# Due times from a backward pass, head-major features, phi on GpSimd and reciprocals on ScalarE in a two-layer linear-attention and gated-MLP kernel

## The chip, the cores and the metric

The kernel runs on one core of a Trainium2 chip. The core has five engines: PE (TensorE, matmuls), DVE (VectorE), ACT (ScalarE), POOL (GpSimd) and SP (SyncE, which issues DMAs here). The metric is the device time of one execution in microseconds; smaller is better.

## The reference

The input is x of 2048 rows and 512 columns. Two layers run, each of an attention block A and a gated MLP block B, both with a residual and a LayerNorm without gain; both layers use the same weights.

```python
qkv = (x @ wqkv).reshape(B, S, 3, H, Dh)...             # H = 32 heads of Dh = 16
pq = einsum("bhsd,hdf->bhsf", q, w_phi)                 # the same for k
phi_q = concat([softmax(pq), softmax(-pq)])             # 32 features a head
kv = einsum("bhsf,bhsd->bhfd", phi_k, v);  z = sum_s phi_k
o  = (phi_q @ kv) / (phi_q @ z + 1e-6)
A  = o.reshape(B, S, D) @ wo
B  = (relu(x @ W_gate) * (x @ W_up)) @ W_down           # F = 1376
x = x + A(ln(x)); x = x + B(ln(x)); x = x + A(ln(x)); x = x + B(ln(x))
```

## The kernel before

The rows are cut into T = 16 tiles of 128. All of x (X, four pieces of four tiles), all weights and the transposed normalized rows (xnTA) stay in SBUF. w_phi is folded into the key and query weights once (`fold`, Wk2 and Wq2: four transposes of the weight on PE, then products with a block-diagonal Wblk).

For a tile of layer l the work is this, with the names under which it stands in the profile:

- `norm_A` (lines 312 to 333): stats and aggr on DVE, Ln and Exp on ACT for the reciprocal standard deviation (rsA), the normalized tile xn on DVE (line 328) or, in layer 0 from tile 2 on, on ACT (line 324, after a small product on DVE, line 321), then a DMA transpose into xnTA issued by SP.
- `Keys.tile` (lines 343 to 390): K (line 348) and V (line 354), four matmuls of 512 columns each; ek, two exponentials on ACT; vext, V copied by ACT; sk, a sum over the 16 features on DVE (line 360); rk, its reciprocal on DVE (line 366); phiK = ek * rk (line 371) on POOL in layer 0 but for the last tile, on DVE otherwise; kvz, eight matmuls of 129 columns that accumulate over all 16 tiles in three PSUM banks. The features of the keys lie feature-major: the 16 features of a head are 8 elements apart.
- `Keys.build`: R, the block-diagonal result, once all 16 tiles are summed.
- `queries`: per four tiles, four groups of four matmuls (line 419) and eight exponentials Eq on ACT. `attend` (lines 429 to 473): eight query matmuls with R (line 437), six copies by ACT (DS, N), six small operations on DVE that end in o, a DMA transpose oT, the projection with wo (line 467) and the residual resA on DVE.
- `mlp` (lines 476 to 538): works on two tiles at once. stats and the centred rows xc (written into the pool xn, line 484), two DMA transposes into xnTB, then for six pairs of the 11 column groups of F the matmuls G and Up (line 504, 256 columns), the copies rg and ru by ACT, their product hT on DVE; then `down` (line 531, 11 matmuls a tile in one piece) and the residual resB on DVE.

The order of the instructions is made by `plan` before anything is emitted. Each operation has an engine, a cost (time that it holds the engine, time until its result), a due time written by hand (TL, STEP, LEAD, ATT in lines 541 to 576), its dependences and the buffers that it takes from pools. `plan` runs a list schedule over the five engines: at every step the engine that can start first takes, among the operations that can start at that time, the one with the smallest due time. Each engine then executes its instructions strictly in that order. PSUM's eight banks are three pools: q (3), a (2: K, Q and the projection) and b (3: V, G, Up, down and the fold). SP issues all loads but wk and wv, all transposes and the stores, in one queue.

## Time and profile before

| | us |
|---|---|
| time of the runs, median of 3 | 440.36 (439.55 to 440.63) |
| the profiled execution, its own time | 439.55 |
| its span, first to last instruction | 437.8 |
| busy PE | 392.7 (90%) |
| busy DVE | 299.8 (68%) |
| busy ACT | 256.6 (59%) |
| busy POOL | 29.4 (7%) |
| mean granted TensorE clock | 0.987 |

The shares are averages over stages with different limits, so the busy time has to be read stage by stage. A row of the stage table gives a stretch of the span; where PE is busy for nearly all of a stretch, only fewer or shorter matmuls shorten it, and elsewhere the wait that ends last has to be found. The groups list all instructions of one line, engine, operation and shape together: count, busy time, the mean of one in ns, and the idle time of the engine ahead of them with its releaser. The chain of waits follows the program back from its last instruction to what released each step.

### The profile page before, as it was taken

What the parts mean: (1) busy time and instruction counts of PE and PEld (TensorE: products, weight loads), DVE (VectorE), ACT (ScalarE), POOL (GpSimd) and SP (SyncE); (2) the same over time, 40 slices, a digit from 0 to 9 for tenths busy, and PEclk for the clock granted to TensorE, in tenths of its full rate; (3) what the DMA queues carried; (4) which work ended last, traced back from release to release, by engine and by line L of the source; (5) the groups of instructions that cost most, each with busy time, mean ns of one, the idle gap of its engine ahead of it and who ended that gap; (6) DMA issues with size and microseconds to landing.
All of it is one profiled execution on the core that took longest, in us unless ns stands there. A gap on an engine that the chain in (4) does not pass through costs nothing.

```text
span 437.8 us, 7642 instructions
## 1 busy us (share of the span) xinstructions
PE 392.7 (90%) x2808; PEld 260.6 (60%) x2848; DVE 299.8 (68%) x687; ACT 256.6 (59%) x631; POOL 29.4 (7%) x21
## 2 busy tenths in 40 slices
PE   1778697899999989989999999877999999999996
PEld 1334344466867555567666654354866868677873
DVE  5599995897799997974746553389956678522222
ACT  3587797993757455554646457966624647335531
POOL 0055572000000000000000000000000000000000
PEclk9999999999999999999999999959999999999999
DMA  8982110251224220100000101003331132200000
GB/s 268 368 209 49 37 36 1 49 72 35 53 49 85 62 49 12 25 0 14 12 14 13 24 1 24 1 12 75 76 69 36 37 76 49 60 13 13 24 25 25
DMA packets 62021, 23.62 MB, mean 54 GB/s; under 512 B 53440, under 2 KB 60960, under 8 KB 61984
## 3 DMA queue, kind: packets, MB, share of 16 engines
q1 hardware_dynamic: 60928, 22.08, 21.4%
q10 hardware_dynamic: 1056, 1.05, 0.8%
q8 instruction: 22, 0.36, 0.4%
q14 instruction: 15, 0.12, 0.1%
HBM read 8.44 MB, written 2.10 MB: 24 GB/s over the span
## 4 chain that ended last, share of the span: by engine, by line
PE 55%; DVE 24%; ACT 8%; DMA 7%; issue 3%; POOL 1%; DVEq 0%; ACTq 0%; SPq 0%
PE b L504 28%; PE b L531 14%; DVE sk L360 9%; PE a L467 4%; PE a L419 3%; ACT Eq L423 3%; DVE rk L366 3%; DVE phiK L371 2%; DMA xnTA<-xn 2%; ACT ek L351 2%; PE q L382 2%; DMA wu<-in_B_W_up_dram 2%; DMA X<-in_A_x_dram 2%; PE a L348 2%; ACT N L444 2%
## 5 line engine op out<-in xcount | busy, mean ns | idle before, releaser
L504 PE MATMUL b<-xnTB,wg 128*128 128x256 bf16 (+1 forms) x704 | 92.5, 273 | 0.5 <-DMA xnTB<-xn 0.4
L504 PE MATMUL b<-xnTB,wu 128*128 128x256 bf16 (+1 forms) x704 | 92.5, 273 | 0.0
L514 ACT ACTIVATE rg<-b 128x512 bf16<-128x512 f32 x96 | 54.7, 570 | 54.4 <-PE b L504 53.6
L531 PE MATMUL b<-wd,hT 128*128 128x512 bf16 (+1 forms) x342 | 78.5, 379 | 0.8
L360 DVE TENSOR_REDUCE sk<-ek 128x64 f32<-128x1024 bf16 x32 | 63.1, 1972 | 19.9 <-ACT ek L351 19.9
L521 DVE TENSOR_TENSOR hT<-rg,ru 128x512 bf16<-128x512 bf16 x96 | 37.7, 394 | 56.6 <-ACT ru L518 56.4
L504 PEld LDWEIGHTS <-wg 128*128 128x128 bf16 (+1 forms) x704 | 69.0, 100 | 12.2 <-DMA xnTB<-xn 0.6
L504 PEld LDWEIGHTS <-wu 128*128 128x128 bf16 (+1 forms) x704 | 69.5, 100 | 9.5 <-issue 0.2
L518 ACT CAST ru<-b 128x512 bf16<-128x512 f32 x96 | 53.2, 554 | 32.7 <-PE b L504 32.2
L531 PEld LDWEIGHTS <-hT 128*128 128x128 bf16 (+1 forms) x352 | 34.4, 98 | 39.8 <-issue 0.3
L444 ACT CAST N<-q 128x384 bf16<-128x384 f32 (+1 forms) x96 | 44.2, 514 | 0.5 <-DVE pr L459 0.5
L351 ACT ACTIVATE ek<-a 128x512 bf16<-128x512 f32 x64 | 35.7, 596 | 11.6 <-PE a L348 11.6
L535 DVE SCALAR_TENSOR_TENSOR X<-b,rsB,X 128x512 bf16<-128x512 f32 x32 | 23.8, 745 | 26.7 <-PE b L531 26.7
L423 ACT ACTIVATE Eq<-a 128x512 bf16<-128x512 f32 x64 | 35.2, 634 | 6.2 <-PE a L419 5.6
L348 PE MATMUL a<-Wk,xnTA 128*128 128x512 bf16 x120 | 32.0, 384 | 5.5 <-DMA xnTA<-xn 5.1
L354 PE MATMUL b<-wv,xnTA 128*128 128x512 bf16 x124 | 33.0, 387 | 3.8 <-DMA xnTA<-xn 2.5
L419 PE MATMUL a<-xnTA,Wq 128*128 128x512 bf16 x122 | 31.3, 378 | 2.5 <-ACT Eq L423 2.1
L444 ACT COPY DS<-q 128x48 f32<-128x48 f32 (+1 forms) x96 | 24.4, 255 | 14.6 <-PE q L437 13.4
L467 PE MATMUL a<-wo,oT 128*128 128x512 bf16 x116 | 30.6, 382 | 1.1 <-DMA oT<-o 0.3
L437 PE MATMUL q<-R,Eq 128*128 128x144 bf16 x256 | 27.4, 240 | 4.6 <-ACT N L444 3.2
L382 PE MATMUL q<-vext,phiK 128*128 128x129 bf16 x256 | 20.6, 224 | 12.0 <-DVE phiK L371 9.0
L371 POOL TENSOR_TENSOR phiK<-ek,rk 128x1024 bf16<-128x1024 bf16 x15 | 28.7, 1911 | 39.0 <-DVE rk L366 27.7
(55 smaller groups left out, 360.1 us busy)
## 6 DMA issues: line engine op xcount, KB each, us to landing
out_dram<-X SPq DMA_DIRECT2D x16, 128.0 KB, 1.7
X<-in_A_x_dram SPq DMA_DIRECT2D x3, 512.0 KB, 7.2
wg<-in_B_W_gate_dram SPq DMA_DIRECT2D x4, 344.0 KB, 7.8
wu<-in_B_W_up_dram SPq DMA_DIRECT2D x4, 344.0 KB, 6.8
wd<-in_B_W_down_dram SPq DMA_DIRECT2D x5, 256.0 KB, 3.6
wk<-in_A_wqkv_dram ACTq DMA_DIRECT2D x1, 512.0 KB, 4.4
wv<-in_A_wqkv_dram ACTq DMA_DIRECT2D x1, 512.0 KB, 5.7
wq<-in_A_wqkv_dram SPq DMA_DIRECT2D x1, 512.0 KB, 7.5
```

The costliest lines, as they stand in the source:

```text
L348: k = op("PE", mm(4, 512), due, lambda: [nc.tensor.matmul(kp.t[:], lhsT=xnTA[c][:, b, cols], rhs=Wk2[:, b, :], start=(b == 0), stop=(b == ...
L351: e = [op("ACT", act(512), due, lambda s=s: nc.scalar.activation(out=ek.t[:, s, :], in_=kp.t[:], func=AF.Exp, scale=1.0 - 2.0 * s), [k], [ ...
L360: a = op("DVE", (1140, 1225), due, lambda: nc.vector.tensor_reduce(out=sk.t[:], in_=ek.t[:].rearrange("p s (b f j) -> p (s b) j f", b=NB, ...
L419: q = op("PE", mm(4, 512), due(c, b), lambda b=b, qp=qp: [nc.tensor.matmul(qp.t[:], lhsT=Wq2[:, m, b * P:(b + 1) * P], rhs=xnTA[c][:, m, : ...
L423: done.append(op("ACT", act(512), due(c, b), lambda b=b, s=s, qp=qp: nc.scalar.activation(out=Eq[c][:, b, s, :], in_=qp.t[:], func=AF.Exp, ...
L444: nc.scalar.copy(out=q[:, k, 0:3] if k < 2 else q[:, :, 3], in_=ps.t[:, 0:n * GE].rearrange("p (n c j) -> p n c j", n=n, j=HB)[:, :, lo:hi])
L467: a = op("PE", mm(4, 512), due + 3, lambda: [nc.tensor.matmul(yp.t[:], lhsT=oT.t[:, b, :], rhs=wo[:, b, :], start=(b == 0), stop=(b == NB ...
L504: nc.tensor.matmul(ps.t[:m, k * 256:(k + 1) * 256], lhsT=W[:, b, g * P:g * P + m], rhs=xT.t[:, b, :], start=(b == 0), stop=(b == NB - 1))
L514: a = op("ACT", act(256 * n), due(0, f), lambda gp=gp, rg=rg, two=two, two_ps=two_ps: nc.scalar.activation(out=two(rg), in_=two_ps(gp), fu ...
L518: u = op("ACT", act(256 * n), due(0, f), lambda up=up, ru=ru, two=two, two_ps=two_ps: nc.scalar.copy(out=two(ru), in_=two_ps(up)), [u], [r ...
L521: lambda rg=rg, ru=ru, two=two, f=f, n=n, w=w: nc.vector.tensor_tensor(out=h.t[:w, f:f + n, :], in0=two(rg), in1=two(ru), op=Alu.mult), [a ...
L531: nc.tensor.matmul(yp.t[:], lhsT=h.t[:m, f, i * P:(i + 1) * P], rhs=wd[:m, f, :], start=(f == 0), stop=(f == NF - 1))
```

## The change

**The planner.** `plan` may now be run several times on the same operations. It gives an operation the smaller due time of those that wait for a buffer of a pool that it holds, counts matmuls at twice their cost for the first 3.5 us, and keeps one clock for DMA traffic. A new function `back` runs the schedule backward, from the last operation, and sets every due time to minus the time that is left behind it; `refine` alternates `plan` and `back` eight times, keeps the due times of the shortest plan and emits that order. The hand-written due times remain as the first round's; their constants are changed, and so are a few costs.

**Features.** The 16 features of a head now lie side by side. sk reads neighbours; Ln and Exp(-x) on ACT turn sk into its reciprocal in place (fp32) instead of DVE's reciprocal; phi multiplies by that fp32 factor, repeated along the features, on POOL in both layers, and half on DVE, half on POOL for the last tile of layer 0 and the last two of layer 1.

**Transposes and norms.** `turn` transposes by DMA or by PE with a copy by ACT or DVE. PE does it for the norms of tiles 0 to 3 in layer 0 and 14 and 15 in layer 1, and for oT and xnTB of tiles 0 and 1 in both layers. xn is always made on DVE.

**MLP blocks.** A block may hold one tile (128 columns; four column groups of F share one bank) or two; the first two blocks of both layers and the last two of layer 1 hold one. `down` is emitted in three pieces, the order alone deciding what stands between them. G and Up of a pair are no longer tied to ACT's copies one by one.

**Loads and banks.** wk comes in two halves, later X in halves, and all other weights one or two pieces after each tile's norm; a warm-up of eight matmuls on zeros is added; pools a and b become one pool of five banks.

```diff
-HOP = {"PE": 50, "ACT": 30, "DVE": 30, "POOL": 165, "SP": 90}
+HOP = {"PE": 50, "ACT": 32, "DVE": 32, "POOL": 165, "SP": 90}
+COLD = 3500
 def plan(ops):
...
+        def rank(o):
+            return min([o.due] + [wanted[b.pool] for b in o.uses + o.takes if b.pool in wanted]), o.n
...
-            pick = min((o for t, o in at if t <= first + 1), key=lambda o: (o.due, o.n))
+            best = first, min((o for t, o in at if t <= first + 1), key=rank)
...
+        if o.eng == "PE":
+            warm = t + COLD if warm is None else warm
+            if t < warm:
+                occ, lat = 2 * occ, lat + occ
+        if o.move:
+            queue = max(t + 1400, queue) + o.move
+            lat = max(lat, queue + 600 - t)
...
+def back(ops):
...
+                at = [(max(clock[e], ready[o] + o.end - o.start - o.spent), o) for o in cand]
...
+        clock[o.eng] = t + o.spent
+        o.due = -clock[o.eng]
...
+def refine(ops, rounds):
...
+    for k in range(rounds):
+        dues = [o.due for o in ops]
+        span = max(o.end for o in plan(ops))
+        if best is None or span < best[0]:
+            best = span, dues
+        back(ops)
...
-POOL_PHI = (2100, 1940)
-XPOSE = (1200, 2470)
+POOL_PHI = (1930, 1940)
+XPOSE = (1200, 2430)
...
+ROUNDS = 8
+BLOCKS = ((1, 1, 2, 2, 2, 2, 2, 2, 2), (1, 1, 2, 2, 2, 2, 2, 2, 1, 1))
...
-    p_q, p_a, p_b = psum("q", 3), psum("a", 2), psum("b", 3)
+    p_q, p_b = psum("q", 3), psum("b", 5)
+    p_a = p_b
...
+    op("PE", mm(8, 512), 0, lambda: [nc.tensor.matmul(
+        wps.t[:], lhsT=p_h.tiles[0][:, 0:P], rhs=p_h.tiles[0][:, 0:512],
+        start=True, stop=True) for _ in range(8)], [c_z], [wps], name="warm")
...
+    def turn(src, dst, how, due, after, takes, uses, name):
+        if how == "SP":
+            return op("SP", XPOSE, due, lambda: nc.sync.dma_start_transpose(out=dst(), in_=src.t[:]), [after],
+                      takes, [src] + uses, name=name, move=500)
+        ps = Buf(p_b)
+        a = op("PE", mm(4, 128), due, lambda: [nc.tensor.matmul(
+            ps.t[:, b * P:(b + 1) * P], lhsT=src.t[:, b * P:(b + 1) * P], rhs=ident[:], start=True, stop=True)
+            for b in range(NB)], [after, c_id], [ps], [src], name=name)
+        return evac(how, due, dst, lambda: ps.t[:].rearrange("p (b t) -> p b t", b=NB), [a], takes, [ps] + uses,
+                    name)
...
-            a = op("DVE", (1140, 1225), due, lambda: nc.vector.tensor_reduce(
-                out=sk.t[:], in_=ek.t[:].rearrange("p s (b f j) -> p (s b) j f", b=NB, j=HB), axis=AX.X,
-                op=Alu.add), e, [sk], [ek], name="sk")
-            def recip():
-                with nc.allow_low_precision("softmax weights are bf16"):
-                    nc.vector.reciprocal(out=rk.t[:], in_=sk.t[:])
-            a = op("DVE", rcp(64), due, recip, [a], [rk], [sk], name="rk")
+            a = op("DVE", SUM16, due, lambda: nc.vector.tensor_reduce(
+                out=sk.t[:], in_=ek.t[:].rearrange("p s (h f) -> p (s h) f", f=DH), axis=AX.X, op=Alu.add), e,
+                [sk], [ek], name="sk")
+            a = op("ACT", (210, 310), due, lambda: nc.scalar.activation(
+                out=sk.t[:], in_=sk.t[:], func=AF.Ln, scale=1.0), [a], (), [sk], name="lnk")
+            a = op("ACT", (110, 220), due, lambda: nc.scalar.activation(
+                out=sk.t[:], in_=sk.t[:], func=AF.Exp, scale=-1.0), [a], (), [sk], name="rk")
+            def phi(e, s, n):
+                e.tensor_tensor(
+                    out=ph.t[:, s:s + n].rearrange("p s (h f) -> p (s h) f", f=DH),
+                    in0=ek.t[:, s:s + n].rearrange("p s (h f) -> p (s h) f", f=DH),
+                    in1=sk.t[:, s * H:(s + n) * H].unsqueeze(2).to_broadcast([P, n * H, DH]), op=Alu.mult)
...
+            for lo, hi in ((0, 4), (4, 8), (8, NF)):
+                def down(yp=yp, i=i, lo=lo, hi=hi):
...
-            nxt.append(norm_A(1, t, s0 + 14000 + 2000 * i, [a], "DVE"))
-            keys.tile(t, max(s0 + 22000 + 2500 * i, TL[0] + ATT * T + 3000 * t), nxt[t], "DVE")
+                    nxt.append(norm_A(1, t, e0 + 2400 * i, [a], "ACT" if t >= T - 2 else "SP"))
+                    keys.tile(t, k0, k0 + p["V0"], k0 + p["Z0"], nxt[t], "POOL" if t < T - 2 else "BOTH",
+                              "DVE" if t >= T - 1 else "ACT")
...
-    order = plan(ops)
+    order = refine(ops, ROUNDS)
```

What the new order does to the queues is shown at three places. The first is SP's queue in the load stage. Before, from the third piece of the gate weight on (wg and wu are the gate and up weights, wo the output weight; the number behind a name is that of a buffer, so xnTA_80 is one of the four pieces of the transposed rows):

```order
L227 DMA wg<-in_B_W_gate_dram 128x1376
L332 DMA_TRANSPOSE xnTA_80<-xn_114 128x4x128
L227 DMA wg<-in_B_W_gate_dram 128x1376
L227 DMA wu<-in_B_W_up_dram 128x1376 x2
L332 DMA_TRANSPOSE xnTA_80<-xn_115 128x4x128
L227 DMA wu<-in_B_W_up_dram 128x1376 x2
L227 DMA wo<-in_A_wo_dram 32x4x512 x4
```

and in the changed kernel, the first transposes on that queue:

```order
L379 DMA_TRANSPOSE xnTA_80<-xn_114 128x4x128
L298 DMA wq<-in_A_wqkv_dram 128x512 x2
L379 DMA_TRANSPOSE xnTA_80<-xn_115 128x4x128
L298 DMA wg<-in_B_W_gate_dram 128x1376 x2
L379 DMA_TRANSPOSE xnTA_80<-xn_116 128x4x128
```

The gate, up and output weights have moved from ahead of the first transposes to places between them, and the transposes of the first four tiles have left the queue.

The second place is DVE among the keys of layer 0. Before (lnA is the small product of line 321 for the next xn on ACT):

```order
L366 RECIPROCAL rk_133<-sk_129 128x64
L321 SCALAR_TENSOR_TENSOR lnA_92<-mvA_90,rsA_91 128x1
L360 TENSOR_REDUCE sk_126<-ek_118 128x64
L321 SCALAR_TENSOR_TENSOR lnA_92<-mvA_90,rsA_91 128x1
L310 BN_AGGR mvA_90<-bstA_89 128x2
L366 RECIPROCAL rk_130<-sk_126 128x64
```

and in the changed kernel, from the second sum on:

```order
L432 TENSOR_REDUCE sk_126<-ek_118 128x64
L392 BN_AGGR mvA_89<-bstA_88 128x2
L432 TENSOR_REDUCE sk_127<-ek_119 128x64
L391 BN_STATS bstA_88<-X_62 128x6
L402 TENSOR_SCALAR xn_114<-X_62,mvA_89,rsA_90 128x512
```

The reciprocals and the small products are gone from DVE, and the normalized tiles, which ACT made, stand between the sums.

The third place is DVE where the keys of layer 1 are made inside the MLP blocks of layer 0 (hT is the product of gate and up). Before:

```order
L360 TENSOR_REDUCE sk_127<-ek_119 128x64
L366 RECIPROCAL rk_131<-sk_127 128x64
L521 TENSOR_TENSOR hT_163<-rg_165,ru_168 128x512
L371 TENSOR_TENSOR phiK_123<-ek_119,rk_131 128x1024
L360 TENSOR_REDUCE sk_128<-ek_120 128x64
L366 RECIPROCAL rk_132<-sk_128 128x64
L371 TENSOR_TENSOR phiK_124<-ek_120,rk_132 128x1024
L521 TENSOR_TENSOR hT_163<-rg_166,ru_169 128x512
```

and in the changed kernel:

```order
L600 TENSOR_TENSOR hT_159<-rg_162,ru_165 128x512
L432 TENSOR_REDUCE sk_127<-ek_119 128x64
L432 TENSOR_REDUCE sk_128<-ek_120 128x64
L600 TENSOR_TENSOR hT_159<-rg_160,ru_163 128x512
L600 TENSOR_TENSOR hT_159<-rg_161,ru_164 128x512
L600 TENSOR_TENSOR hT_159<-rg_162,ru_165 96x256
```

The two sums of a block now stand together, and what followed each of them on DVE, rk and phiK, is done by ACT and POOL beside the products that follow.

More of the change, by code (lines that the diff above doesn't have):

```diff
@@ L61, in __init__ @@
         self.tiles = tiles
-        self.free = [(0.0, i) for i in range(len(tiles))]
-HOP = {"PE": 50, "ACT": 30, "DVE": 30, "POOL": 165, "SP": 90}
+HOP = {"PE": 50, "ACT": 32, "DVE": 32, "POOL": 165, "SP": 90}
+COLD = 3500
 def plan(ops):
-    for n, o in enumerate(ops):
-        o.n = n
-        o.left = len(o.deps)
-        o.ready = 0.0
-        for d in o.deps:
-            d.then.append(o)
-    clock = dict.fromkeys(HOP, 0.0)
+    for o in ops:
+        o.left, o.ready, o.room = len(o.deps), 0.0, []
+        for b in o.takes + o.uses:
+            b.users, b.end = 0, 0.0
+            b.pool.free = [(0.0, i, None) for i in range(len(b.pool.tiles))]
+    for o in ops:
+        for b in o.takes + o.uses:
+            b.users += 1
+    clock = dict.fromkeys(HOP, 700.0)
+    queue, warm = 0.0, None
     open_ = {e: [o for o in ops if o.eng == e and not o.left] for e in HOP}
@@ L254, with load_next @@
+    late += [("u", wu[:, b, :], uv[:, b, :], 352256) for b in range(NB)]
+    late += [("d", wd[:, f:f + 2, :], dv[:, f:f + 2, :], 262144) for f in range(0, 10, 2)]
+    late += [("d", wd[:96, 10, :], B_W_down[10 * P:F, :], 98304)]
+    homes = dict(q=l_wq, g=l_wg, o=l_wo, u=l_wu, d=l_wd)
+    def load_next(after, due):
+        if late:
+            kind, dst, src, nbytes = late.pop(0)
+            homes[kind].append(load(due, dst, src, nbytes, deps=[after]))
     c_id = op("POOL", (900, 900), 0, lambda: make_identity(nc, ident[:]), name="ident")
@@ L341, in __init__, with tile @@
             self.sums = []
-        def tile(self, t, due, xT, phi_eng):
+        def tile(self, t, due, due_v, due_z, xT, phi_eng, v_eng="ACT"):
             c, i = t // C, t % C
@@ L546 @@
     for t in range(T):
-        xT.append(norm_A(0, t, 2000 + 2300 * t, [x_in[t]], "DVE" if t < 2 else "ACT"))
-        keys.tile(t, 10000 + 2300 * t, xT[t], "POOL" if t < T - 1 else "DVE")
+        if t == 2:
+            x_in[2] = load(4, X[0][:, 2, :], xv[:, 2, :], 131072, deps=[x_in[0]])
+            x_in[3] = load(5, X[0][:, 3, :], xv[:, 3, :], 131072, deps=[x_in[0]])
+        if t >= 4 and t % 2 == 0:
+            x_in[t] = x_in[t + 1] = load(
+                p["K0"] + p["KS"] * (t - 5), X[t // C][:, t % C:t % C + 2, :], xv[:, t:t + 2, :], 262144,
+                deps=[xT[t - 4]])
@@ new lines @@
+        xT.append(norm_A(0, t, p["K0"] - 4000 + p["KS"] * t, [x_in[t]], ("ACT", "DVE")[t % 2] if t < 4 else "SP"))
+        if t >= 3:
+            load_next(xT[t], p["K0"] + p["KS"] * t)
+            load_next(xT[t], p["K0"] + p["KS"] * t)
+        k0 = p["K0"] + p["KS"] * t
+        keys.tile(t, k0, k0 + p["V0"], k0 + p["Z0"], xT[t], "POOL" if t < T - 1 else "BOTH")
+    while late:
+        load_next(xT[-1], p["K0"] + p["KS"] * T)
+    q_fold = fold(wq, Wq2, l_wq, p["QF"], 100, ("ACT", "DVE"))
```

379 lines of the change are left out of this document (204 added, 175 removed).

## The prediction

> **What bounds the kernel now.** First the busy time by stage, cut where the chain of waits changes its leader. The columns are the stretch, its length, then busy us and instructions of PE, PE's weight loads, DVE, ACT and POOL, the granted clock, the DMA share and GB/s.
>
> ```profile
> 0.00:21.50 21.50, 9.29 (x53) 5.78 (x55) 12.00 (x38) 8.58 (x21) 0.70 (x6) 1.00 0.98 317
> 21.50:70.20 48.70, 37.98 (x266) 19.77 (x269) 47.52 (x61) 39.87 (x90) 28.67 (x15) 1.00 0.35 77
> 70.20:92.50 22.30, 19.96 (x130) 10.82 (x133) 16.00 (x54) 20.74 (x65) 0.00 (x0) 1.00 0.17 37
> 92.50:150.00 57.50, 56.55 (x436) 40.81 (x440) 48.86 (x145) 33.29 (x98) 0.00 (x0) 1.00 0.32 59
> 150.00:257.50 107.50, 101.15 (x743) 68.11 (x751) 77.69 (x131) 59.18 (x126) 0.00 (x0) 1.00 0.09 19
> 257.50:305.30 47.80, 39.74 (x222) 21.01 (x226) 27.11 (x70) 33.81 (x98) 0.00 (x0) 0.89 0.11 23
> 305.30:434.20 128.90, 128.01 (x964) 94.33 (x976) 69.84 (x193) 61.15 (x137) 0.00 (x0) 1.00 0.18 43
> ```
>
> In rows four and seven PE is busy for 56.55 of 57.50 us and 128.01 of 128.90 us: 186 us that only less matmul work could shorten, and the change removes none. PE can gain in the other rows alone: the load stage, the keys of layer 0 (DVE 47.52 of 48.70 us), its queries (ACT 20.74 of 22.30), the keys of layer 1 inside the MLPs (row five) and the passage to layer 1 (row six, where the granted clock falls as well).
>
> **The start.** The chain of waits (start, us, what) and the timeline there (start, us, engine, line, what):
>
> ```profile
> 19.76 5.02 DMA xnTA<-xn
> 5.39 0.69 DVE L267 TENSOR_TENSOR Wblk<-wf,M 128x512 bf16<-128x512 bf16 x1 [1.41 <-DMA wf<-in_A_w_phi_dram]
> 20.44 1.08 ACT L351 ACTIVATE ek<-a 128x512 bf16<-128x512 f32 x2 [3.39 <-PE a L348]
> 15.53 1.52 ACT L324 ACTIVATE xn<-X,lnA,rsA 128x512 bf16<-128x512 bf16 x2 [0.29 <-DVE lnA L321]
> 279.20 3.28 ACT L423 ACTIVATE Eq<-a 128x512 bf16<-128x512 f32 x6
> 92.57 0.87 PE b L504 x8
> ```
>
> The first exponential of the keys starts at 20.44, and transposes are late: the chain waits 5.02 us for one, issued behind weight loads on SP. Tiles 0 to 3 now turn on PE. The groups that follow (line, engine, operation, count, then busy us and the mean ns of one) price what DVE and ACT do there and later:
>
> ```profile
> L280 PE MATMUL b<-ident,wk 128*128 128x128 bf16 x16 | 1.9, 311 | 5.2 <-DMA wk<-in_A_wqkv_dram 5.2
> L288 DVE CAST wT<-b 128x512 bf16<-128x512 f32 x4 | 2.7, 676 | 0.0
> L309 DVE BATCH_NORM_STATS2 bstA<-X 128x6 f32<-128x512 bf16 x32 | 21.6, 684 | 3.0 <-DMA X<-in_A_x_dram 2.6
> L328 DVE TENSOR_SCALAR xn<-X,mvA,rsA 128x512 bf16<-128x512 bf16 x18 | 7.3, 404 | 6.5 <-ACT rsA L317 6.5
> L324 ACT ACTIVATE xn<-X,lnA,rsA 128x512 bf16<-128x512 bf16 x14 | 11.3, 814 | 5.8 <-DVE lnA L321 5.4
> L315 ACT ACTIVATE lnA<-mvA,eps 128x1 f32<-128x1 f32 x32 | 9.5, 299 | 35.1 <-DVE mvA L310 34.3 <-DVE rsB L492 0.9
> L317 ACT ACTIVATE rsA<-lnA 128x1 f32<-128x1 f32 x32 | 6.4, 201 | 0.3
> L444 ACT CAST N<-q 128x384 bf16<-128x384 f32 (+1 forms) x96 | 44.2, 514 | 0.5 <-DVE pr L459 0.5
> L444 ACT COPY DS<-q 128x48 f32<-128x48 f32 (+1 forms) x96 | 24.4, 255 | 14.6 <-PE q L437 13.4 <-PE a L467 0.6 <-DVE w L456 0.3
> ```
>
> and PE's pace: from the chain a projection of four matmuls of 512 columns, from the timeline kvz (129 columns; its weight loads, back to back) and the query matmuls (144 columns):
>
> ```profile
> 161.62 0.86 PE b L354 x4
> 194.97 0.40 PEld L382 LDWEIGHTS <-phiK 128*128 128x128 bf16 x7 [0.77 <-DVE phiK L371]
> 83.29 0.82 PE L437 MATMUL q<-R,Eq 128*128 128x144 bf16 x8
> 83.95 0.81 PE L419 MATMUL a<-xnTA,Wq 128*128 128x512 bf16 x3
> ```
>
> Now DVE sets the first key. Wblk ends at 5.39 + 0.69 = 6.1, since the same load releases it; then one xn (0.40), two casts (0.68 each), one copy of folded weights, one stats and the last copy (2 x 0.68 + 0.68) give 9.9, and a K projection (0.86) gives the first exponential at 10.8, 9.6 us earlier.
>
> From there ACT decides. From 21.5 to 92.5 it is busy 39.87 + 20.74 = 60.6 of 71 us, 85%. It loses twelve xn (two of the 14 run at 15.53): 12 x 0.81 = 9.7. It gains Ln and Exp for 16 reciprocals. The trace has these on one column only, 0.30 + 0.20; 64 columns cannot cost less, and at most the 0.81 of a 512-column pass (xn's row) each. I take the one-column rows, the nearer, 16 x 0.50 = 8.0, and keep 16 x 1.6 = 26 as the other end. Four evacuations of transposes of 512 columns add 4 x 0.55 = 2.2 (an Eq of that width, 3.28 / 6). In the new order 43 instead of 59 query matmuls stand ahead of the first gate matmul, two tiles whose six copies take 3 x (0.26 + 0.51) = 2.3: minus 4.6. That leaves 56.5 us, at the same 85% 66.5 us, so the first gate matmul starts at 10.8 + 66.5 = 77.3 instead of 92.57. PE then still owes three projections and 16 query matmuls, 3 x 0.86 + 16 x 0.08 = 3.9 us. **Net minus 11.4**; with Ln and Exp at 19 us no gain is left, at the dear end it is 10 slower.
>
> DVE must not be what holds this up instead:
>
> ```profile
> L492 DVE RECIPROCAL rsB<-lnB 128x2 f32<-128x2 f32 x16 | 2.4, 152 | 0.2
> L360 DVE TENSOR_REDUCE sk<-ek 128x64 f32<-128x1024 bf16 x32 | 63.1, 1972 | 19.9 <-ACT ek L351 19.9
> L263 DVE TENSOR_REDUCE Mf<-ident 128x8 f32<-128x128 bf16 x1 | 0.4, 366 | 0.0
> L261 DVE TENSOR_REDUCE M<-ident 128x8 bf16<-128x128 bf16 x1 | 0.3, 286 | 0.3 <-POOL ident masks.py:199 0.3
> L366 DVE RECIPROCAL rk<-sk 128x64 bf16<-128x64 f32 x32 | 17.6, 550 | 1.4
> L371 DVE TENSOR_TENSOR phiK<-ek,rk 128x1024 bf16<-128x1024 bf16 x17 | 11.6, 685 | 0.5
> L371 POOL TENSOR_TENSOR phiK<-ek,rk 128x1024 bf16<-128x1024 bf16 x15 | 28.7, 1911 | 39.0 <-DVE rk L366 27.7 <-DVE lnA L321 6.0 <-PE q L382 3.7
> ```
>
> Lines 261 and 263 reduce the same 128 elements, 261 with neighbours in memory, 263 with strides: 286 against 366 ns. With the 0.15 us that an operation on two columns takes (line 492), that is 1.06 and 1.69 ns an element; 1024 of the second make 1.88 us, close to the 1.97 measured. Head-major features turn sk into the first kind: 1024 x 1.06 + 150 = 1.24 us. DVE saves 0.73 on sk and 0.55 on rk, and pays 0.40 for xn, about 0.9 us a tile, 14 of its 47.5 us: ACT is the bound. phi on POOL with an fp32 factor repeated along its innermost axis has no row; its neighbours are DVE's 0.69 below, POOL's 1.91, and above it 1.91 x 1.6 = 3.1 if that layout slows POOL as strides slow DVE. I take POOL's own 1.91; at 3.1, 15 in a row with xn between take 52 us and add about 6.
>
> The other start edits I cost at nothing. The weights now go out between the transposes; a transpose may again take the 5.02 above for 2.4, but xn is made four tiles ahead (cover gone: 2.6 us each). One pool of five banks and paced X loads only loosen waits; the eight warm-up matmuls run while the first loads arrive.
>
> **Keys of layer 1.** The waits of PE from 150 to 257.5 (who waited, for what: total us, times, longest):
>
> ```profile
> PE q L382 <- DVE phiK L371: 5.1, 7, 1.5
> ```
>
> PE's idle time there is 107.50 - 101.15 = 6.35. In the new order both K and V of a block stand five G/U groups ahead of kvz, so phi has 5 us on POOL. DVE loses 0.73 + 0.55 + 0.68 a tile, 27 of its 77.69 us for some 14 tiles. I take back 4 of the 6.35, the rest going to the lock below. **Minus 4.**
>
> **The passage.** The chain, then from the timeline the two centred tiles of the first block:
>
> ```profile
> 286.07 0.70 DVE phiK L371
> 302.65 2.66 DMA xnTB<-xn
> 299.88 0.35 DVE L484 TENSOR_SCALAR xn<-X,mvB 128x512 bf16<-128x512 bf16 x1
> 302.28 0.35 DVE L484 TENSOR_SCALAR xn<-X,mvB 128x512 bf16<-128x512 bf16 x1
> ```
>
> Between the start of the last phi and that of the first gate matmul, where row six ends, lie 19.2 us. A one-tile first block need not wait for the second xn: 302.28 - 299.88 = 2.4. A transpose on PE with its copy takes about 4 x 0.12 + 0.55 + 0.1 of hand-overs = 1.1 instead of 2.66: twice 1.5. The last sk is 0.73 shorter. Three query groups move ahead, six Eq of 0.55 on ACT, though their 3 x 0.86 = 2.6 us of matmuls move too: 0.7. That is 6.8; I take **minus 6.5**, since the last phi, half on DVE and half on POOL, is no shorter; if those two exclude each other it is 1 longer.
>
> **What it adds on PE.** Fourteen transposes of 4 x 0.12 = 0.5, about half in full stretches: 3.5. Six one-tile blocks run 88 matmuls at 128 columns; the nearest rows are kvz, 7 weight loads in 0.40 us, and the query matmuls, 8 from 83.29 to the next group at 83.95. That is 0.057 or 0.082 us each, against half of a 256-column matmul, 0.87 / 16 = 0.0545 by the x8 row at 92.57. I take the nearer kvz: 6 x 88 x 0.0025 = 1.3; the other end is 14.5. **Plus 5.** Splitting the down projection adds no matmul. The tail behind the last stretch, the last store, stays.
>
> **Sum.** -11.4 - 4 - 6.5 + 5 = -17 on the profiled execution's 439.55 us (span 437.8 and 1.75 around it; the median 440.36 is 0.8 above): 422.5, and **422** is the forecast.
>
> **Rivals.** *The lock (slower).* One row of the timeline shows DVE held by POOL:
>
> ```profile
> 46.80 1.91 POOL L371 TENSOR_TENSOR phiK<-ek,rk 128x1024 bf16<-128x1024 bf16 x1 [1.72 <-ACT ek L351]
> 47.07 1.66 DVE L321 SCALAR_TENSOR_TENSOR lnA<-mvA,rsA 128x1 f32<-128x1 f32 x1
> ```
>
> An operation on one column, with two tensors from SBUF, lasted 1.66 us and ended at 48.73, 0.02 after POOL's phi. If every DVE operation of that kind, and xn too, must wait out a phi, then a tile whose xn comes just behind the start of phi costs sk 1.24 + Ln and Exp 0.50 + phi 1.91 + xn 0.40 = 4.05 us, 16 of them 65, 16 us more than the 48.7 of row two, of which the start 9.6 earlier pays all but 7; behind the blocked xn stand stats and the next sk, for which ACT and PE wait. In the MLPs 14 phis hold an hT for up to 1.91, half of it on the path, 13, and the 4 won there are gone. 439.55 + 7 + 13 - 6.5 + 5 gives **458**. It decides if xn meets phi in over half of the tiles; where it falls between two phis, POOL's 1.91 + 0.40 = 2.3 a tile stays under ACT's pace, which is why I give it less. The Trainium skill, "SBUF — State Buffer", section "Who interferes with whom", says that a DVE instruction with two SBUF inputs, or in a two-port mode, and a GpSimd instruction that reads SBUF exclude each other for whole instructions; the row above agrees for two inputs, and no run here shows xn against POOL. By that rule hT, pr, o and xn all take part.
>
> *ACT or PE pays more.* Ln and Exp at 19 us instead of 8, or 128-column matmuls at 0.082: the start's gain or 13 us are lost, **434**. *More is won*: ACT at 95% instead of 85% brings the first gate matmul to 70.5, 7 us more, and all 6.35 of row five go, **413**. *Nothing*: the planner's new order starves PE elsewhere by what the start wins, **440**.
>
> **Chances.** Forecast 0.47 (own range 414 to 430), ACT or PE 0.17, more 0.17, nothing 0.05, the lock 0.14. The range leaves the lock out and a sliver below: 407 to 440. A measurement of this kernel tells 0.3%, 1.3 us, from no change: faster 0.81, same 0.05, slower 0.14.
>
> **What would show it.** Right: sk near 1.24 us, POOL's phi near 1.9, the first exponential near 11, the first gate matmul near 78, no wait of PE for phi, some 13 us from last phi to first gate matmul in layer 1, stretches of full PE afterwards. Wrong: xn or hT lasting over 1 us while phi runs; Ln of 64 columns over 0.4; gate matmuls of 128 columns spaced over 0.07; a transpose behind weights that holds K.

## The result, and the profile after

The changed kernel takes **411.14 us** (median of 4 runs, 410.80 to 412.41) against 440.28 (439.55 to 440.63) of the kernel before on the same chip. The ratio is 0.9345, with a 95% interval of 0.9322 to 0.9369: 29 us faster. The forecast was 422 with a range of 407 to 440, so the sign and the range held and the gain was put 11 us too small.

In the profiled execution the span fell from 437.8 to 409.6 us. The busy line of the page after:

```profile
PE 389.8 (95%) x3176; PEld 266.2 (65%) x3176; DVE 267.8 (65%) x656; ACT 258.1 (63%) x704; POOL 61.9 (15%) x38
```

PE was idle for 437.8 - 392.7 = 45.1 us before and is idle for 409.6 - 389.8 = 19.8 us now: 25.3 of the 28.2 us are idle time of PE that went. The busy time by stage after, in the columns of the prediction's first table, cut at the first gate matmul of each layer and where PE stops waiting:

```profile
0.00:73.70 73.70, 64.98 (x472) 35.59 (x473) 59.01 (x118) 61.96 (x181) 31.16 (x22) 1.00 0.54 137
73.70:98.00 24.30, 23.59 (x289) 18.32 (x289) 23.60 (x88) 21.02 (x76) 0.00 (x0) 1.00 0.33 62
98.00:137.60 39.60, 34.86 (x256) 23.67 (x254) 36.59 (x102) 19.71 (x54) 4.11 (x2) 1.00 0.36 68
137.60:243.50 105.90, 105.90 (x777) 73.98 (x778) 55.04 (x83) 58.30 (x140) 19.80 (x10) 0.98 0.07 15
243.50:256.80 13.30, 12.92 (x82) 6.56 (x80) 9.50 (x15) 12.30 (x34) 5.70 (x4) 1.00 0.00 1
256.80:274.20 17.40, 15.78 (x129) 9.48 (x127) 12.95 (x41) 16.49 (x55) 1.17 (x1) 1.00 0.05 9
274.20:405.70 131.50, 131.42 (x1182) 98.56 (x1181) 69.95 (x214) 68.30 (x170) 0.00 (x0) 1.00 0.19 42
```

Up to the first gate matmul PE's idle time fell from 92.5 - 67.2 = 25.3 us (rows one to three of before) to 8.7. The stretch with the keys of layer 1 is now full (row four; before, 6.35 us idle). The passage to layer 1 (rows five and six) has 2.0 us idle at a clock of 1.00, where row six of before had 8.06 at 0.89. Row three is a new loss: DVE is busy for 36.59 of 39.60 us, and PE is idle for 4.7, most of it in one wait. From the timeline, SP's queue and PE at its end (start, us, engine, line, what, and in brackets the idle time before it and its releaser):

```profile
132.49 2.50 SPq L379 DMA_TRANSPOSE xnTA<-xn  x2
135.09 1.22 SPq L379 DMA_TRANSPOSE xnTB<-xn  x1
137.57 1.39 PE L582 MATMUL b<-xnTB,wg 128*128 128x256 bf16 x8 [3.32 <-DMA xnTB<-xn]
```

The transpose that PE waits for is issued behind two others, and all three could only go when DVE had made their rows. The wait costs more than its 3.32 us: the stage row for the four us behind it shows a granted clock of 0.57, some 4 x 0.43 = 1.7 us of PE's pace, and the next eight gate matmuls take 1.39 us instead of the 1.04 of those just before it.

```profile
138.00:142.00 4.00, 4.00 (x23) 3.25 (x22) 0.42 (x1) 1.56 (x3) 0.00 (x0) 0.57 0.00 0
```

The groups that answer to the prediction's prices (line, engine, operation, count, busy us, mean ns, idle before):

```profile
L432 DVE TENSOR_REDUCE sk<-ek 128x64 f32<-128x1024 bf16 x32 | 38.4, 1212 | 19.1 <-ACT ek L424 18.7
L435 ACT ACTIVATE sk<-sk 128x64 f32<-128x64 f32 x32 | 8.5, 265 | 3.0 <-DVE sk L432 2.6
L437 ACT ACTIVATE sk<-sk 128x64 f32<-128x64 f32 x32 | 8.5, 265 | 0.1
L441 POOL TENSOR_TENSOR phiK<-ek,sk 128x1024 bf16<-128x1024 bf16 x29 | 56.7, 1971 | 194.8 <-ACT sk L437 87.8 <-PE b L582 54.7 <-issue 27.8
L402 DVE TENSOR_SCALAR xn<-X,mvA,rsA 128x512 bf16<-128x512 bf16 x32 | 17.6, 561 | 2.8 <-ACT rsA L399 2.6
L600 DVE TENSOR_TENSOR hT<-rg,ru 128x512 bf16<-128x512 bf16 x77 | 44.2, 577 | 61.2 <-ACT ru L596 59.4 <-ACT rg L593 1.6
```

The sum sk takes 1.21 us (forecast 1.24), Ln and Exp 0.53 together (0.50), a whole phi on POOL 1.97 (1.91). But xn takes 561 ns on average where it took 404: the lock of the first rival is real. The timeline among the keys of layer 0 shows one event:

```profile
32.53 1.93 POOL L441 TENSOR_TENSOR phiK<-ek,sk 128x1024 bf16<-128x1024 bf16 x1 [2.12 <-ACT sk L437]
32.60 2.01 DVE L402 TENSOR_SCALAR xn<-X,mvA,rsA 128x512 bf16<-128x512 bf16 x1
```

An xn that starts 0.07 us behind POOL's phi lasts 2.01 us and ends 0.15 us after it. In the timeline four of the 16 xn of layer 0 last about 0.9 us or more too long, and none of layer 1, where the longest takes 0.415; the rival needed over half of the tiles.

### The profile page after: what moved, and what is told of

The parts are those of the page before. It is cut to its first block, busy times and chain, and to the rows that moved or that the text cites. A ratio compares the mean times of both kernels' runs of the same rounds, so it can differ in the third digit from the quotient of the medians.

```text
span 409.6 us, 8406 instructions
## 1 busy us (share of the span) xinstructions
PE 389.8 (95%) x3176; PEld 266.2 (65%) x3176; DVE 267.8 (65%) x656; ACT 258.1 (63%) x704; POOL 61.9 (15%) x38
## 4 chain that ended last, share of the span: by engine, by line
PE 61%; DVE 17%; ACT 7%; issue 3%; DMA 2%; DVEq 0%; SPq 0%; POOL 0%; ACTq 0%; POOLq 0%
PE b L582 31%; PE b L614 16%; PE b L421 3%; DVE bstB L391 3%; PE b L427 3%; ACT Eq L497 3%; PE b L540 2%; DVE X L544 2%; PE q L456 2%; PE b L493 2%; DVE pr L533 2%; DMA xnTA<-xn 1%; ACT ek L424 1%; DVE o L536 1%; DVE xn L558 1%
## 5 line engine op out<-in xcount | busy, mean ns | idle before, releaser
L593 ACT ACTIVATE rg<-b 128x512 bf16<-128x512 f32 (+1 forms) x102 | 55.7, 553 | 82.0 <-PE b L582 80.8
L582 PE MATMUL b<-xnTB,wg 128*128 128x256 bf16 (+3 forms) x836 | 93.5, 257 | 5.0 <-DMA xnTB<-xn 3.3
L582 PE MATMUL b<-xnTB,wu 128*128 128x256 bf16 (+3 forms) x836 | 93.9, 257 | 0.0
L600 DVE TENSOR_TENSOR hT<-rg,ru 128x512 bf16<-128x512 bf16 (+1 forms) x102 | 50.2, 500 | 64.7 <-ACT ru L596 62.9
L441 POOL TENSOR_TENSOR phiK<-ek,sk 128x1024 bf16<-128x1024 bf16 (+1 forms) x32 | 61.2, 1930 | 195.4 <-ACT sk L437 87.8
L596 ACT CAST ru<-b 128x512 bf16<-128x512 f32 (+1 forms) x102 | 54.2, 537 | 25.6 <-PE b L582 23.5
L432 DVE TENSOR_REDUCE sk<-ek 128x64 f32<-128x1024 bf16 x32 | 38.4, 1212 | 19.1 <-ACT ek L424 18.7
L424 ACT ACTIVATE ek<-b 128x512 bf16<-128x512 f32 x64 | 35.0, 607 | 11.7 <-PE b L421 11.7
L497 ACT ACTIVATE Eq<-b 128x512 bf16<-128x512 f32 x64 | 39.4, 666 | 2.3 <-PE b L493 2.2
L421 PE MATMUL b<-Wk,xnTA 128*128 128x512 bf16 x128 | 32.1, 380 | 4.3 <-DMA xnTA<-xn 3.3
L540 PE MATMUL b<-wo,oT 128*128 128x512 bf16 x128 | 32.7, 379 | 1.2 <-ACT Eq L497 0.9
```

What stands on the lines that cost most here:

```text
L421: k = op("PE", mm(4, 512), due, lambda: [nc.tensor.matmul(kp.t[:], lhsT=xnTA[c][:, b, cols], rhs=Wk2[:, b, :], start=(b == 0), stop=(b == ...
L441: e.tensor_tensor(out=ph.t[:, s:s + n].rearrange("p s (h f) -> p (s h) f", f=DH), in0=ek.t[:, s:s + n].rearrange("p s (h f) -> p (s h) f", ...
L497: done.append(op("ACT", act(512), due(c, b), lambda b=b, s=s, qp=qp: nc.scalar.activation(out=Eq[c][:, b, s, :], in_=qp.t[:], func=AF.Exp, ...
L540: a = op("PE", mm(4, 512), due + 3, lambda: [nc.tensor.matmul(yp.t[:], lhsT=oT.t[:, b, :], rhs=wo[:, b, :], start=(b == 0), stop=(b == NB ...
L582: nc.tensor.matmul(ps.t[:m, q * W:(q + 1) * W], lhsT=w[:, b, g * P:g * P + m], rhs=xT.t[:, b, 0:W], start=(b == 0), stop=(b == NB - 1))
L593: a = op("ACT", act(cols), due_g(f0), lambda gp=gp, rg=rg, lo=lo, hi=hi, m=m: nc.scalar.activation(out=part(rg, lo, hi, m), in_=part(gp, l ...
```

## The experiments

Each kernel was compared with the kernel before on the same chip. The last three columns are the start of the first gate matmul in layer 0, that in layer 1, and the end of the last matmul (us, from the timeline of PE in each profiled execution). The chain of waits, which the prediction used, has the first gate matmul of before at 92.57. Work may cross these borders, so the totals decide and the columns tell where. The planner runs anew in each kernel, so a run shows the edit together with the order that it leads to. The kernel before took 440.5 to 440.7 us (medians) beside the experiments and 440.28 beside the change, so a difference of under 1 us between two medians below says nothing.

| kernel | median us | ratio (95% interval) | gate, layer 0 | gate, layer 1 | last matmul |
|---|---|---|---|---|---|
| before | 440.28 | | 92.4 | 305.4 | 434.1 |
| after | 411.14 | 0.9345 (0.9322 to 0.9369) | 73.7 | 274.2 | 406.1 |
| e1_no_back | 436.84 | 0.9903 (0.9886 to 0.9920) | 84.0 | 298.7 | 431.7 |
| e2_old_keys | 422.38 | 0.9579 (0.9561 to 0.9597) | 89.1 | 284.0 | 415.9 |
| e3_dma_passage | 408.07 | 0.9258 (0.9243 to 0.9274) | 77.1 | 270.6 | 402.5 |
| e4_pairs | 411.34 | 0.9337 (0.9301 to 0.9372) | 77.8 | 271.0 | 404.7 |
| e5_keys_only | 434.19 | 0.9860 (0.9821 to 0.9899) | 94.2 | 300.6 | 429.1 |
| e6_plan_only | 419.49 | 0.9522 (0.9483 to 0.9560) | 92.0 | 288.8 | 415.5 |
| e7_phi_dve | 407.77 | 0.9253 (0.9219 to 0.9288) | 73.6 | 270.0 | 402.0 |
| e8_one_back | 414.70 | 0.9410 (0.9354 to 0.9467) | 77.8 | 278.0 | 409.9 |
| e9_other_order | 412.17 | 0.9341 (0.9302 to 0.9381) | 74.9 | 277.1 | 409.1 |
| e10_queries_first | 415.53 | 0.9424 (0.9388 to 0.9461) | 73.9 | 278.6 | 411.5 |
| e11_phi_all_dve | 414.14 | 0.9398 (0.9369 to 0.9427) | 82.3 | 276.5 | 408.4 |
| e12_both | 406.64 | 0.9224 (0.9198 to 0.9251) | 76.5 | 269.5 | 401.4 |

**What the order alone is worth.** The first kernel keeps every operation of the change and emits the first round's plan, made from the due times written by hand.

```diff
-ROUNDS = 8
+ROUNDS = 1
```

> The changed kernel with one planning round instead of eight: the due times written by hand stay, nothing else changes. If the gain of 29 us comes from the cheaper work of the keys and the passages (theory of the prediction), most of it stays: 414 to 418 us, first gate matmul within 3 us of 73.7. If it comes from the order (rival: the backward pass puts query groups and MLP work under the waits), 424 us or more, with idle PE in the passage to layer 1 as before (8 us or more between the last kvz and the first gate matmul).

Measured 436.84: the rival, and by more than it asked. Of 29 us, about 25 go: 10.3 at the start, 14.2 between the two first gate matmuls. Two rows of its stage table (the columns as above) show the second loss:

```profile
84.00:150.00 66.00, 58.34 (x506) 41.06 (x513) 57.82 (x178) 35.19 (x107) 3.87 (x2) 0.95 0.30 57
263.00:298.70 35.70, 27.61 (x158) 15.28 (x158) 19.44 (x51) 20.71 (x69) 3.01 (x2) 0.81 0.02 4
```

PE idles for 7.7 and 8.1 us there, and in the passage the granted clock is 0.81, after 0.89 before the change. The idle time does not lie where it was expected: between the last key product and the first gate matmul it is 1.4 us, the rest stands ahead of that product.

e8 stops after one backward pass, the shorter of two plans.

```diff
-ROUNDS = 8
+ROUNDS = 2
```

> The changed kernel with two rounds of the planner: one backward pass, and the shorter of the two plans. Theory, what matters is that due times count what is left behind an operation, and one pass gives that: 411 to 416. Rival, the gain needs the alternation, as due times and order have to agree: 420 to 430.

Measured 414.70, the theory: one pass gives 22 us of what e1 lost, the six other rounds 3.6. e9 runs on to 24 rounds and ends with another order that the planner holds to be equally long.

```diff
-ROUNDS = 8
+ROUNDS = 24
```

> The changed kernel with 24 rounds instead of eight: the planner ends with another order whose planned length is within 0.02 us of the one it had. Theory, orders of equal planned length take equal time within about 1.3 us, so the 3 us that e3 and e7 won come from their edits: 410 to 412.5. Rival, the order alone scatters by as much as those two won: under 408.5 or over 414.

Measured 412.17, inside the theory's 410 to 412.5; by the ratio (0.9341 against 0.9345) it does not differ from the change at all. One such pair was tried, so that totals 3 us apart come from their edits and not from a chance of the order is likely, not shown. The columns scatter more: in its profiled execution, the slowest of its four (414.52), the first gate matmul of layer 1 comes 2.9 us later than in the change.

**The planner alone, the keys alone.** e6 is the kernel before with the new planner and nothing else but sk's cost in it.

```diff
-            a = op("DVE", (1140, 1225), due, lambda: nc.vector.tensor_reduce(
+            a = op("DVE", (1890, 1985), due, lambda: nc.vector.tensor_reduce(
...
-    order = plan(ops)
+    order = refine(ops, 8)
```

> The kernel before with the new planner alone (plan, back and refine with eight rounds, and sk's cost put at its measured 1.9 us); operations, keys, transposes, blocks, banks and loads as before. Theory, the backward pass is the main lever on any set of operations, since without it the changed kernel falls back to 436.8: 418 to 426. Rival, it pays only together with the new keys, transposes and banks, because the old keys hold DVE for 47 of 49 us: 430 to 440.

Measured 419.49, the theory: 21 us. None of it is at the start (first gate matmul 92.0 against 92.4); 16.2 lie between the first gate matmuls. Its stage rows there:

```profile
0.00:92.00 92.00, 69.34 (x452) 38.30 (x461) 76.68 (x154) 69.66 (x177) 29.24 (x21) 0.96 0.46 124
150.00:258.00 108.00, 107.36 (x789) 73.61 (x798) 78.54 (x138) 62.39 (x134) 0.00 (x0) 1.00 0.11 22
258.00:288.80 30.80, 27.04 (x183) 14.78 (x184) 25.40 (x67) 29.03 (x89) 0.00 (x0) 1.00 0.18 35
```

With the old keys inside the MLPs, DVE as busy as before (78.54 us), PE idles 0.6 us instead of 6.35. The new order alone removes these waits, without lightening DVE. The corrected cost of sk was not run by itself; it is part of these 21 us.

e5 is the kernel before with the new keys alone.

```diff
-            a = op("DVE", (1140, 1225), due, lambda: nc.vector.tensor_reduce(
-                out=sk.t[:], in_=ek.t[:].rearrange("p s (b f j) -> p (s b) j f", b=NB, j=HB), axis=AX.X,
+            a = op("DVE", (1140, 1225), due, lambda: nc.vector.tensor_reduce(
+                out=sk.t[:], in_=ek.t[:].rearrange("p s (h f) -> p (s h) f", f=DH), axis=AX.X,
...
+            a = op("ACT", (210, 310), due, lambda: nc.scalar.activation(
+                out=sk.t[:], in_=sk.t[:], func=AF.Ln, scale=1.0), [a], (), [sk], name="lnk")
...
-            keys.tile(t, max(s0 + 22000 + 2500 * i, TL[0] + ATT * T + 3000 * t), nxt[t], "DVE")
+            keys.tile(t, max(s0 + 22000 + 2500 * i, TL[0] + ATT * T + 3000 * t), nxt[t], "POOL" if t < T - 2 else "BOTH")
```

> The kernel before with the new keys alone (head-major features, Ln and Exp on ACT, phi on POOL in both layers, the last ones split), old planner, old due times, old transposes. Theory, the parts add up: taking the new keys out of the changed kernel cost 11 us, so putting them into the one before wins about as much, 427 to 433. Rival, the room that they leave on DVE is only used by an order that is made for it: no more than 4 us are won, 436 to 441.

Measured 434.19: between the two, some 6 us, and again none at the start (94.2). In the stretch with the keys of layer 1 PE now idles 2.4 us instead of 6.35, in the old order:

```profile
150.00:257.50 107.50, 105.09 (x773) 71.61 (x783) 64.23 (x106) 65.30 (x158) 27.21 (x14) 1.00 0.10 20
```

So the lighter DVE removes 3.9 us of these waits by itself, as the new order removes 5.7 of them by itself. They are the same waits, and the two gains do not add.

e2 goes the other way, the changed kernel with the old keys, phi of layer 1 on DVE as it was.

```diff
-                out=sk.t[:], in_=ek.t[:].rearrange("p s (h f) -> p (s h) f", f=DH), axis=AX.X, op=Alu.add), e,
+                out=sk.t[:], in_=ek.t[:].rearrange("p s (b f j) -> p (s b) j f", b=NB, j=HB), axis=AX.X,
...
+                    nc.vector.reciprocal(out=rk.t[:], in_=sk.t[:])
...
-                    keys.tile(t, k0, k0 + p["V0"], k0 + p["Z0"], nxt[t], "POOL" if t < T - 2 else "BOTH",
+                    keys.tile(t, k0, k0 + p["V0"], k0 + p["Z0"], nxt[t], "DVE",
```

> The changed kernel with the old keys: features feature-major, sk strided at 1.97 us, reciprocal on DVE at 0.55, phi on DVE in layer 1 at 0.69 and on POOL in layer 0; the planner is told these costs. Theory of the prediction: the start is DVE's again, 16 x (0.73 + 0.55) = 20 us more on DVE there, some of it under ACT: first gate matmul at 83 to 88 instead of 73.7, and in the MLPs of layer 0 waits for phi of 1 to 3 us: 421 to 428 us. Rival (order): the planner hides the dearer sums, 412 to 417 us.

Measured 422.38, inside the theory's range. Two of its signs missed: the first gate matmul falls back from 73.7 to 89.1, a little beyond the 83 to 88 expected, and its trace lists no wait of PE for phi, where 1 to 3 us were expected in the MLPs of layer 0. Between the two first gate matmuls e2 is even 5.6 us shorter than the change (194.9 against 200.5): in the new order, what the new keys win lies at the start alone. The row among the keys of layer 0 shows DVE full again:

```profile
21.50:70.20 48.70, 40.67 (x252) 21.17 (x255) 47.03 (x59) 34.47 (x84) 20.99 (x11) 0.93 0.60 158
```

On the old code neither the new keys (e5) nor the new order (e6) moves the start. e1, which has keys, loads, banks and transposes without the backward pass, wins 8.4 of the 18.7 us; e2, which has all of the change but the new keys, wins 3.3. How much of the start the loads and the transposes of tiles 0 to 3 bring was not run by itself.

**The passage.** e10 puts all query groups of layer 1 ahead of the last key product, where they stood before the change.

```diff
+        if l == 1:
+            keys.sums[-1].deps += [o.deps[0] for e in eq for o in e]
```

> The changed kernel with all 16 query groups of layer 1 ordered before the last key product (one more dependence, nothing else), as they stood before the change. Theory, the passage was won because 13 query groups now run behind the last key product and fill the chain to the first gate matmul, whose length is the same as before: idle time of PE comes back there, 4 to 8 us, 415 to 419. Rival, it was won by a shorter chain (one-tile first block, transposes on PE), as predicted: the queries' place matters little, 410 to 413.

Measured 415.53, the theory's side, 4.4 us above the change. Most of that comes from the queries' place, not all: in e10's profiled execution the clock falls for longer than in the change behind the wait near 137 us, which costs 1.7 us more. The one run of e10 whose mean granted clock was 0.996, as in three of the change's four, took 413.81, 2.8 us more than they. (The timeline has 28 query matmuls, seven groups, behind the last key product, not 13; before the change and in e10 there is none.) From the start of the last phi to the first gate matmul the stage tables say, in this order for before, after, e10 and e1:

```profile
286.10:305.30 19.20, 14.91 (x103) 9.96 (x104) 16.76 (x55) 13.08 (x55) 0.00 (x0) 0.73 0.20 43
```

```profile
256.50:274.20 17.70, 16.02 (x130) 9.72 (x131) 13.25 (x41) 16.79 (x56) 1.47 (x2) 1.00 0.04 9
```

```profile
264.20:278.50 14.30, 11.73 (x99) 7.80 (x99) 11.91 (x40) 12.68 (x47) 1.54 (x2) 0.88 0.05 9
```

```profile
283.20:298.70 15.50, 12.81 (x88) 8.90 (x90) 11.85 (x38) 10.63 (x43) 1.50 (x1) 0.67 0.04 8
```

With no query in it the chain did become shorter, 19.2 to 14.3 or 15.5, though less than to the forecast's 12.7. The changed kernel's is longer, 17.7, because PE does 130 matmuls in it instead of 99, at full clock.

e4 and e3 take back the parts that were to shorten the chain. e4 makes every block of two tiles:

```diff
-BLOCKS = ((1, 1, 2, 2, 2, 2, 2, 2, 2), (1, 1, 2, 2, 2, 2, 2, 2, 1, 1))
+BLOCKS = ((2,) * 8, (2,) * 8)
```

> The changed kernel with two-tile MLP blocks throughout. Theory of the prediction: the first gate matmul of each layer waits for a second tile, 2.4 us each: 414 to 417 us, the 128-column matmuls having cost next to nothing. Rival: the one-tile blocks bring nothing (the wait is filled) or cost PE time: 409 to 412 us.

Measured 411.34, the rival: with or without one-tile blocks the time is the same, within 1.6 us (its interval). e3 sends xnTB of tiles 0 and 1 in both layers and the last two norms of layer 1 by DMA again:

```diff
-                       "ACT" if t0 < 2 else "SP")
+                       "SP")
...
-                    nxt.append(norm_A(1, t, e0 + 2400 * i, [a], "ACT" if t >= T - 2 else "SP"))
+                    nxt.append(norm_A(1, t, e0 + 2400 * i, [a], "SP"))
```

> The changed kernel with xnTB of tiles 0 and 1 of both layers and xnTA of tiles 14 and 15 of layer 1 transposed by DMA instead of PE and ACT. Theory of the prediction: each such step on the chain of a passage costs 1.5 us more, one in layer 0's start and two in the passage to layer 1, less 1 us of PE work: 414 to 416 us. Rival: the passage is no longer bound by its chain, since query groups fill it: within 1.3 us of 411.

Measured 408.07, below both ranges (theory 414 to 416, rival within 1.3 us of 411): making these six transposes on PE, with the order that goes with it, costs 3 us in place of gaining any.

**The lock.** e7 puts phi of layer 1 on DVE, in one piece, so that POOL does nothing beside the MLPs.

```diff
-                    keys.tile(t, k0, k0 + p["V0"], k0 + p["Z0"], nxt[t], "POOL" if t < T - 2 else "BOTH",
+                    keys.tile(t, k0, k0 + p["V0"], k0 + p["Z0"], nxt[t], "DVE",
```

> The changed kernel with the phi of layer 1 on DVE in one piece (about 2 us each, since the half takes 1.03): no POOL work beside the MLPs, so no hT is held by POOL there. Theory, the 12 us by which POOL held hT cost nothing, since PE was full there, and DVE has room for 16 x 2 us: 409 to 415. Rival, the lock does cost PE time and this takes it away: 400 to 407.

Measured 407.77, between the two and 3.4 us faster than the change. Groups of e7, and its row for the stretch where DVE was full:

```profile
L600 DVE TENSOR_TENSOR hT<-rg,ru 128x512 bf16<-128x512 bf16 x77 | 32.0, 417 | 60.6 <-ACT ru L596 58.9 <-ACT rg L593 1.6
L441 DVE TENSOR_TENSOR phiK<-ek,sk 128x1024 bf16<-128x1024 bf16 x16 | 19.1, 1213 | 0.0
```

```profile
98.00:137.60 39.60, 36.85 (x279) 26.45 (x282) 34.21 (x102) 21.83 (x56) 0.00 (x0) 1.00 0.35 64
```

hT is back at 417 ns. So POOL held hT for (577 - 417) x 77 = 12.3 us, and phi on DVE costs 19.1 us of its time. Where PE is full (137.6 to 243.5) neither matters. Between 98 and 137.6 it does: the changed kernel ran two phis on POOL there. One held a small product of an attend, the other a small operation of an MLP norm, from the timeline:

```profile
102.93 2.19 POOL L441 TENSOR_TENSOR phiK<-ek,sk 128x1024 bf16<-128x1024 bf16 x1 [42.98 <-PE b L582]
103.25 1.92 DVE L526 TENSOR_TENSOR m<-m 128x32 f32<-128x32 f32 x1
123.47 1.93 POOL L441 TENSOR_TENSOR phiK<-ek,sk 128x1024 bf16<-128x1024 bf16 x1 [18.35 <-ACT sk L437]
123.94 1.48 DVE L563 TENSOR_SCALAR lnB<-mvB 128x2 f32<-128x2 f32 x1
```

Elsewhere in the stretch these take 0.16 to 0.19 and 0.14 to 0.17 us, so some 3 us are lost, and DVE has no gap there until 134.9 in which to make up for it. In e7 DVE has 34.21 instead of 36.59 us of work there, with two phis of its own in it, and PE gets 36.85 us done instead of 34.86. Its wait for the transpose is 2.49 us instead of 3.32, and the clock behind it stays at 1.00. The clock is part of the gain, not all: the runs with a mean granted clock of 0.996 differ by 2.6 us (three of the change, two of e7). That the two holds caused the longer wait is likely, but e7's order differs as well, and this was not separated.

e11 takes the phi of layer 0 from POOL as well.

```diff
-        keys.tile(t, k0, k0 + p["V0"], k0 + p["Z0"], xT[t], "POOL" if t < T - 1 else "BOTH")
+        keys.tile(t, k0, k0 + p["V0"], k0 + p["Z0"], xT[t], "DVE")
```

> The changed kernel with every phi on DVE, in layer 0 as well: no POOL work and no lock anywhere. In e7 phi took 1.21 us on DVE. Theory, in the keys of layer 0 DVE has no such room (59 of 73.7 us busy, and 15 x 1.2 less the 5 us of the lock make 72): the first gate matmul comes 4 to 10 us later than in e7, 411 to 418. Rival, ACT is the bound there and the lock hid the rest: as e7, 406 to 410.

Measured 414.14, the theory: 6.4 us more than e7, the first gate matmul 8.7 us later. In layer 0, where phi on DVE would come on top of 59.0 busy us in 73.7, POOL earns its place in spite of the lock.

**Both.** e12 joins the edits of e7 and e3.

> The changed kernel with phi of layer 1 on DVE (e7) and the transposes of xnTB and of the last two norms by DMA (e3). Theory, the two gains have different places (DVE held by POOL in the first MLP blocks, extra matmuls and a late block behind them) and add up: 403.5 to 406. Rival, both free the same stretch from 98 to 138 us, where DVE is full, and only one counts: 407 to 409.

Measured 406.64, between the two ranges: beside e3's 3.1 and e7's 3.4 the two together win 4.5 us. They seem to share part of what they free, but 2 us are about the noise of three such differences, so that is not shown. Its median is the lowest of all kernels here, 4.5 us below the change, though its interval overlaps those of e3 and e7.

## Why the prediction was right, and where it was off

**Right.** The reading of before: the gain lies where PE waits. Of the start, mechanism and terms. The first exponentials in the timeline of after, and a row of its stage table from the forecast's 10.8 to the first gate matmul:

```profile
10.02 1.07 ACT L424 ACTIVATE ek<-b 128x512 bf16<-128x512 f32 x2
```

```profile
10.80:73.70 62.90, 56.78 (x420) 31.39 (x419) 51.38 (x94) 55.94 (x169) 30.46 (x16) 1.00 0.51 123
```

The first exponential starts at 10.0 (forecast 10.8), and ACT is busy for 55.9 us (forecast 56.5). Only the 85% was mis-sized: ACT reached 55.94 / 62.90 = 89%, so the first gate matmul came at 73.7, not 77.3, 3.6 us more gain. The prices of sk, Ln and Exp, and phi on POOL were all within 6%. PE's wait for phi, 5.1 us before in the MLPs, is almost gone (waits of PE over the whole span: who waited, for what, total us, times, longest):

```profile
PE q L456 <- POOL phiK L441: 0.4, 1, 0.4
```

The "minus 4" for the keys of layer 1 was right for the old order, where e5 wins 3.9 of the 6.35 us by DVE's lighter load. In the change it brings nothing of its own, since e6 wins 5.7 of them by the order and e2, without the new keys, loses nothing there.

**How near, and by what luck.** The measurement lies outside the forecast's own 414 to 430, nearest to the rival "More is won" at 413. That rival asked for ACT at 95%, a first gate matmul at 70.5 and all 6.35 us of row five; measured were 89% and 73.7, and of the 6.35 none is left. But its sum, like the forecast's, is made of the operations, and these without the backward pass were worth about 4 us (e1), less than the 17 forecast. That the time still came out inside the stated range is in part luck: the order, which had no term, paid for what the terms put too high.

**The rival of the lock** described a mechanism that exists: xn, hT and the small products are all held. The Trainium skill, "SBUF — State Buffer", section "Who interferes with whom", has the rule that the prediction cites, by which the one of the two that starts later is blocked until the other has ended; the prediction had no run of xn against POOL, and the 2.01 us above now agree with it. The rival's price was wrong for this kernel: xn lost (561 - 404) x 32 = 5.0 us in all, in four tiles for the most part, where the rival let every tile wait and the stage grow by 16, and most of the 12.3 us of hT fell where PE was full. What phi of layer 1 on POOL did cost, 3.4 us net of DVE's 19.1 (e7), shows in a place that the rival did not name, the small operations in the first MLP blocks.

**The step that failed** is the passage, "minus 6.5" as a shorter chain, with "Three query groups move ahead" for 0.7. The chain by itself became shorter by 3.7 to 4.9 (e1, e10; the granted clock in it differs as well, 0.67 and 0.88 against 0.73), but the one-tile blocks, put at 2.4 of that, can be taken away at no loss (e4), and the transposes on PE, put at 3.0, cost time where e3 takes some of them back. No query group stood behind the last key product before, so none was there to move ahead; what the step missed is that the order could put seven of them into the chain, worth about 3 to 4 us (e10). More widely, the forecast took its terms from the operations and gave the backward due times no term of their own; with the operations alone the kernel stands at 436.8 (e1), and the planner on the old operations gives 419.5 (e6).

**Plus 5 on PE**: the 128-column matmuls were priced rightly. Two groups of 16 from the timeline start 0.89 us apart, 0.056 us a matmul where the forecast took 0.057, and e4 shows no cost:

```profile
276.09 1.06 PE L582 MATMUL b<-xnTB,wg 128*128 128x128 bf16 x16
276.98 1.06 PE L582 MATMUL b<-xnTB,wu 128*128 128x128 bf16 x16
```

The six transposes of e3 cost 3.1 in all. How much of that is work of PE and how much their places in the queues was not separated.

## What to carry to other kernels

When a list schedule runs on hand-written due times, try due times from a backward pass before any new operation: here it was 21 us on the old code and about 25 of 29 with the new, and one pass gave most. An idle engine is not free where its work holds up a busy one: price a move to it by that as well, stage by stage, since the same phi belonged on POOL in layer 0 and on DVE in layer 1. And a part that shortens a chain can be worth nothing once other work fills that chain.
